# Balancing two batches by sums on ScalarE, with a new order of work from the start of mixing

## The chip, the cores and the metric

The kernel runs on one core of a Trainium2 chip. It uses TensorE (PE, matrix products), VectorE (DVE), ScalarE (ACT), GpSimd (POOL) and the queue of SyncE (SP), which starts most of the transfers. The metric is the device time of one execution in microseconds (us).

## The reference

All arrays are seeded random numbers; q, k, v are (4 batches, 4 heads, 1088 positions, 32), and the attention features come from two 8 x 32 matrices S1, S2.

```python
def phi(x):                                   # 64 features of each position
    a = np.einsum('rd,bhsd->bhsr', S1, x)
    b = np.einsum('rd,bhsd->bhsr', S2, x)
    return np.einsum('bhsi,bhsj->bhsij', a, b).reshape(*x.shape[:-1], r * r)
q_p, k_p = (phi(q), phi(k))
kv = np.einsum('bhsf,bhsd->bhfd', k_p, v)
z = np.sum(k_p, axis=2)
num = np.einsum('bhsf,bhfd->bhsd', q_p, kv)
den = np.einsum('bhsf,bhf->bhs', q_p, z)[..., None] + 1e-06
x = num / den                                 # then as (batch, position, 128)
theta = x @ w_theta
zr, zi = x * np.cos(theta), x * np.sin(theta)
y = w_tok_r @ zr + w_tok_i @ zi               # mixes the 1088 positions
u = x + y
out = u + np.maximum(u @ w_ch, 0.0)
```

## The kernel before

**Stages.** Positions are cut into chunks of 128 (nine, the last one short), 128 on the partitions. For each batch the kernel forms sums over keys ("keys", "sums", "rest"), a small chain of 32x32 and 128x128 products on them ("chain"), kv ("kf", "kv"), the scaled and rounded queries ("qT", "q0"), the two factors of the denominator ("levels", "den"), the numerator ("num"), theta with its cosine and sine ("theta"), and then mixes positions: w_tok stands as 17 rows of 128 x 1088 (eight real, eight imaginary, one with the ends of both), each loaded as 8-byte words into a buffer of class "zs" and turned into floats by two ScalarE activations (L576, L578) and two VectorE steps (L580, L582). Batches 0 and 1 are mixed row by row ("mix", L1197): for each row three products of up to 384 columns add into three PSUM banks. Batches 2 and 3 (PAIR) are mixed together by seven products of half matrices (function winograd, "m1" to "m7"), for which VectorE makes sums and differences of the w_tok rows and of the two batches' z. The last step, u + relu(u @ w_ch), and the stores are in finish.

**The join.** For batches 1 to 3 the keys k are taken apart into a rounded part kb and a rest r. The "rest" products (L680) are of r with k + kb. That sum, kh, is not made by an engine: k is loaded a second time into kh, and a transfer issued by POOL adds kb to it in place (function join, L326, called in key_sums, stage "keys"). There are 9 x 4 narrow products (32 columns on 32 output partitions); L682 then puts the result's two "corners" together by 32x32 products.

**The turn.** For batches 1 to 3 (XTURN) x is not transposed by PE: VectorE transposes 32x32 blocks (L1097), SP sends the result to a place in HBM ("far", L1098) and fetches it back in another order (L1102).

**The balance.** Before batches 2 and 3 are mixed together, batch 3 is scaled by a power of two near the ratio of the two batches' magnitudes, partition by partition. balance() (L1166) puts a magnitude of each batch into columns 0 and 1 of the tile even, takes the powers of two (ratio, L1172), and leaves the factor in column 4 and its inverse in column 5. ScalarE scales batch 3 by it ahead of its turn (L1092). Scaling and its inverse are both exact, so only the size of rounding errors hangs on the choice.

**What sets the order.** The functions do not issue instructions; they record 1001 operations with their engine, buffers and predecessors. The tuple ORDER lists all operations, and issue() emits them in that order; each engine then runs its own part of the list strictly in order and waits on semaphores where an input or a buffer is not ready. GAPS says where small idle products are put on PE as a filling, SLOTS which physical buffer each logical one takes: a buffer can be written only when the last user of the one before it in its place is through, so SLOTS adds waits of its own. "zs" has five places, which w_tok's raw rows, z, and the turn's tiles share. Mixing begins on PE at 57 us with rows 0, 1, 2 of batch 0.

Of the kernel before, what the change touches and what calls it, by code (L numbers as in the profile page):

```python
# [11 lines left out]
BF16 = mybir.dt.bfloat16  # L12
# [5 lines left out]
AF = mybir.ActivationFunctionType  # L18
ALU = mybir.AluOpType
AX = mybir.AxisListType  # L20
PSUM = bass.MemoryType.PSUM

P = 128
# [54 lines left out]
)  # L78
GAPS = {11: 3, 57: 3, 79: 3, 110: 1, 203: 8, 153: 1, 77: 5, 86: 2, 163: 1}
SLOTS = (  # L80
# [11 lines left out]
)  # L92
WARM = 0
LOAD_LEAD = 60.0
# [37 lines left out]
class Layout:  # L132
# [17 lines left out]
    def buf(self, cls, shape, dt, name):  # L150
        b = Buf(cls, shape, dt, name)
        self.bufs.append(b)
        return b
# [75 lines left out]
def dve(n):  # L229
    return (n + 145) / 960.0  # L230


def dve2(n):
    return (n / 2 + 150) / 960.0


def act(n):
    return 0.17 + 0.00083 * n
# [7 lines left out]
def kernel(  # L246
# [12 lines left out]
    B, _, NC, H, D = q.shape  # L259
# [38 lines left out]
    op, buf = L.op, L.buf  # L298

    def at(*name):  # L300
        L.stage = "".join(str(x) for x in name)

    V, A, G, T, SY = nc.vector, nc.scalar, nc.gpsimd, nc.tensor, nc.sync

    def fixed(shape, dt, name):
        b = Buf(None, shape, dt, name)
        n = math.prod(shape) * WORD[dt]
        b.ap = view(const.tile([P, (n + 3) // 4], F32, tag=name, name=name), shape, dt)
        return b
# [4 lines left out]
    def ts(o, a, s1, op0, s2=None, op1=None, eng=None):  # L314
        kw = {} if op1 is None else {"op1": op1}
        (eng or V).tensor_scalar(out=o, in0=a, scalar1=s1, scalar2=s2, op0=op0, **kw)  # L316

    def stt(o, a, s, b, op0, op1, eng=None):
        (eng or V).scalar_tensor_tensor(out=o, in0=a, scalar=s, in1=b, op0=op0, op1=op1)  # L319
# [8 lines left out]
    def vop(n, fn, w, r, due=None, two=False, lk=0):  # L328
        op("V", dve2(n) if two else dve(n), fn, w, r, due, lk=1 if two else lk)
# [80 lines left out]
    def powers(mfn, m, n, name):  # L410
# [7 lines left out]
        def inv():  # L418
# [16 lines left out]
                                    op=ALU.max, apply_absolute_value=True), [m2], [(sp, 0)])  # L435
# [476 lines left out]
    qs, qx, q0, xT, zt = {}, {}, {}, {}, {}  # L912
    even = fixed((6,), F32, "even")
# [109 lines left out]
    def outputs_x(b, lv, pool_qp):  # L1023
# [60 lines left out]
        if b == PAIR[1]:  # L1084
            src = balance()
# [80 lines left out]
    def balance():  # L1166
        at("even")
        for j, b in enumerate(PAIR):
            vop(NC * P, lambda j=j, b=b: V.tensor_reduce(out=even()[:, j:j + 1], in_=xT[b](), axis=AX.X, op=ALU.max,
                                                         apply_absolute_value=True), [(even, j)], [xT[b]])  # L1170

        def ratio():  # L1172
            e = even()
            ts(e[:, 0:2], e[:, 0:2], TINY, ALU.max, 1.0 / TINY, ALU.min)
            ei = e.bitcast(I32)
            ts(ei[:, 2:4], ei[:, 0:2], EXPO, ALU.bitwise_and, EXPO, ALU.bitwise_xor)
            ts(ei[:, 0:2], ei[:, 0:2], EXPO, ALU.bitwise_and)
            stt(e[:, 4:5], e[:, 0:1], 0.5, e[:, 3:4], ALU.mult, ALU.mult)
            stt(e[:, 5:6], e[:, 1:2], 0.5, e[:, 2:3], ALU.mult, ALU.mult)

        op("V", 0.85, ratio, [even], [], lk=5)
        return even
# [300 lines left out]
```

## Time and profile before

| | before |
|---|---|
| median of 3 runs | 217.91 us (217.88 to 218.24) |
| the profiled execution | 217.77 us |
| its span, first to last instruction | 216.0 us |
| granted TensorE clock, mean | 0.997 |
| busy: PE, DVE, ACT, POOL | 207.4, 180.7, 113.5, 38.5 us |
| moved by DMA | 37.06 MB |

A row of a timeline or of the chain has the start, the time it takes (both us), engine, line, operation, output and inputs, and their shapes; x says how many instructions or records are merged into it. A float32 product appears as two records. A row of groups ends in "busy us, mean ns | idle before". A matmul's end is modelled, and the records of consecutive products overlap: PE's real pace is the distance from start to start. Lines are those of the kernel before; the changed kernel has one line more from L1169 on.

### The profile page before, as it was taken

How to read it: one execution, taken by the hardware profiler on the slowest of the kernel's cores; microseconds unless marked ns; L12 is line 12 of the kernel's file. 1: busy time of each engine (PE TensorE's matmuls, PEld its weight loads, DVE VectorE, ACT ScalarE, POOL GpSimd, SP SyncE). 2: the span in 40 equal slices, each digit the busy share in tenths (PEclk: the TensorE clock that was granted, in tenths of full speed). 3: DMA queues.
4: the chain of work that ended last, by engine and by line, in shares of the span. 5: the costliest groups of instructions: out<-in, count | busy, mean ns of one | idle time of the engine just before them, and what ended most of it. 6: DMA issues, size and time to landing. Idle time of an engine off the chain costs nothing.

```text
span 216.0 us, 5299 instructions
## 1 busy us (share of the span) xinstructions
PE 207.4 (96%) x2140; PEld 150.2 (70%) x2140; DVE 180.7 (84%) x359; ACT 113.5 (53%) x240; POOL 38.5 (18%) x89
## 2 busy tenths in 40 slices
PE   7999999999999999999999999999999999999990
PEld 7777798968767666775656676576766776677660
DVE  1799999999999998998999999979497799955151
ACT  4899999999999896796711423159500000000000
POOL 1182640307300000930003010000220020020013
PEclk9999999999999999999999999999999999999998
DMA  6999999996996994192002244022660012110433
GB/s 226 395 417 418 380 362 420 429 324 143 347 244 230 421 429 177 56 323 49 0 0 36 40 141 113 0 39 108 137 109 0 0 39 50 17 36 4 76 62 67
DMA packets 28044, 37.06 MB, mean 172 GB/s; under 512 B 20564, under 2 KB 23044, under 8 KB 25844
## 3 DMA queue, kind: packets, MB, share of 16 engines
q1 hardware_dynamic: 22868, 31.86, 42.2%
q0 software_dynamic: 1552, 3.25, 7.1%
q10 hardware_dynamic: 3600, 1.62, 2.8%
q8 instruction: 17, 0.28, 0.5%
q14 instruction: 7, 0.06, 0.1%
HBM read 29.84 MB, written 4.00 MB: 157 GB/s over the span
## 4 chain that ended last, share of the span: by engine, by line
PE 58%; DMA 17%; DVE 10%; ACT 9%; issue 3%; SPq 1%; POOL 0%; POOLq 0%; DVEq 0%; ACTq 0%
PE ps L332 54%; DMA zs<-w_tok 11%; DMA zs<-far 2%; DMA st<-s 2%; DVE big L312 2%; ACT big L578 2%; PE ps L951 2%; ACT big L626 2%; DMA far<-zs 1%; DVE g L312 1%; PE ps L1053 1%; DVE big L316 1%; ACT g L726 1%; ACT big L576 1%; PE ps L361 1%
## 5 line engine op out<-in xcount | busy, mean ns | idle before, releaser
L332 PE MATMUL ps<-big,zs 128*128 128x384 f32 (+2 forms) x380 | 108.8, 435 | 0.0
L332 PEld LDWEIGHTS ps<-big,zs 128*128 128x128 f32 x380 | 67.1, 191 | 34.2 <-issue 0.9
L1281 ACT COPY g<-ps 80x256 f32<-80x256 f32 x1 | 0.4, 367 | 54.1 <-PE ps L1274 54.1
L332 PE MATMUL ps<-big,big 128*32 128x32 f32 (+2 forms) x352 | 21.8, 235 | 0.0
L312 DVE CUSTOM_DVE_ANT_0 big<-big,big 128x2176 uint16<-128x2176 uint16 x17 | 21.6, 1281 | 0.1
L578 ACT ACTIVATE big<-zs 128x1088 int32<-128x1088 uint32 (+1 forms) x18 | 21.3, 1190 | 0.7 <-DMA zs<-w_tok 0.7
L576 ACT ACTIVATE big<-zs 128x1088 f32<-128x1088 f32 x17 | 20.9, 1229 | 0.7 <-DMA zs<-w_tok 0.7
L332 PEld LDWEIGHTS ps<-big,big 128*32 128x32 f32 (+1 forms) x352 | 14.9, 125 | 5.6 <-issue 1.0
L312 DVE TENSOR_TENSOR big<-big,big 128x544 f32<-128x544 f32 x24 | 16.7, 713 | 0.1
L326 POOL DMA_DIRECT2D g<-big x6 | 5.3, 1070 | 56.0 <-ACT g L1213 56.0
L1236 POOL DMA_DIRECT2D out<-g x8 | 5.0, 631 | 50.3 <-DVE g L1240 36.0
L312 DVE TENSOR_TENSOR zs<-zs,g 128x384 f32<-128x384 f32 (+2 forms) x24 | 9.9, 449 | 4.0 <-DMA zs<-far 4.0
L316 DVE TENSOR_SCALAR big<-big 128x1088 int32<-128x1088 int32 x17 | 12.3, 721 | 0.0
L361 PE MATMUL ps<-idle 128*128 128x112 bf16 (+1 forms) x67 | 10.0, 312 | 1.3 <-POOL idle L363 1.3
L312 DVE TENSOR_TENSOR g<-lv 128x768 f32<-128x768 f32 x12 | 11.1, 950 | 0.1
L312 DVE TENSOR_TENSOR big<-big,hf 128x1152 f32<-128x1152 f32 x8 | 10.7, 1351 | 0.0
L332 PE MATMUL ps<-mf,big 128*128 128x96 f32 (+1 forms) x72 | 10.0, 278 | 0.4 <-DVE big L312 0.4
L332 PE MATMUL ps<-sbk,g 128*128 128x64 f32 x72 | 10.1, 276 | 0.3 <-ACT g L726 0.3
L332 PE MATMUL ps<-w,big 128*128 128x128 f32 (+1 forms) x76 | 10.2, 278 | 0.0
L332 PEld LDWEIGHTS ps<-w,big 128*128 128x128 f32 (+1 forms) x76 | 9.4, 190 | 0.5
L1139 ACT ACTIVATE g<-g 128x384 f32<-128x384 f32 x12 | 6.3, 532 | 6.7 <-DVE g L319 6.7
L332 PEld LDWEIGHTS ps<-sbk,g 128*128 128x128 f32 x72 | 9.0, 191 | 0.8 <-ACT g L726 0.6
(198 smaller groups left out, 353.0 us busy)
## 6 DMA issues: line engine op xcount, KB each, us to landing
zs<-w_tok SPq DMA_DIRECT2D x17, 1088.0 KB, 10.6
big<-k_l SPq DMA_DIRECT2D x5, 576.0 KB, 12.6
big<-v_l SPq DMA_DIRECT2D x4, 576.0 KB, 15.4
big<-q_l SPq DMA_DIRECT2D x3, 576.0 KB, 10.4
big<-hf POOLq DMA_DIRECT2D x3, 576.0 KB, 9.7
far<-zs SPq DMA_DIRECT2D x3, 576.0 KB, 3.8
zs<-far SPq DMA_DIRECT2D x12, 144.0 KB, 4.1
big<-k_l ACTq DMA_DIRECT2D x2, 576.0 KB, 4.2
```

The lines of the kernel that those rows point to most:

```text
L312: eng.tensor_tensor(out=o, in0=a, in1=b, op=f)
L316: (eng or V).tensor_scalar(out=o, in0=a, scalar1=s1, scalar2=s2, op0=op0, **kw)
L326: op("G", 0.9, lambda: G.dma_start(dst(), src(), accum_op=ALU.add), w, r, fly=fly)
L332: T.matmul(o, lhs, rhs, start=start, stop=stop, skip_group_check=True)
L361: T.matmul(nowhere()[:, :n], idle()[:, 0:P], idle()[:, :n], start=True, stop=True, skip_group_check=True)
L576: op("A", 0.22 + n * 0.0009, lambda: A.activation(dfn(), words_of(raw(), n)[1].bitcast(F32), AF.Prelu, scale=2.0**-112, alpha=-(2.0**32)), ...
L578: op("A", 0.22 + n * 0.0009, lambda: A.activation(stp(), words_of(raw(), n)[0].bitcast(U32), AF.Copy, scale=2.0**-29), [stp], [raw])
L626: op("A", act(n) + 0.1, lambda: A.activation(flat(r()), kc(), AF.Square, accum_out=km()[:, 1:2]), [r, (km, 1)], [kx])
L726: op("A", act(GW), lambda kT=kT, tr=tr: A.copy(kT().rearrange("p c n -> p (c n)"), tr()), [kT], [tr])
L951: T.transpose(tr()[:, i * P:(i + 1) * P], x()[:, g * GC + i].rearrange("p h d -> p (h d)"), ident())
L1139: op("A", act(GW), lambda cs=cs: A.activation(cs()[:, 0], cs()[:, 1], AF.Abs), [(cs, 0)], [(cs, 1)])
L1236: E.dma_start(out[b, s0:s0 + n, f * SQ:(f + 1) * SQ].rearrange("(c j) i -> j c i", j=SQ), ot()[f * SQ:(f + 1) * SQ, :n].rearrange("j (c i) ...
```

## The change

One part is in balance: in place of VectorE's largest magnitude of x along each partition stands ScalarE's sum of magnitudes, an activation Abs with an accumulated output, whose full output goes to a scratch tile of the class "hf".

```diff
         for j, b in enumerate(PAIR):
-            vop(NC * P, lambda j=j, b=b: V.tensor_reduce(out=even()[:, j:j + 1], in_=xT[b](), axis=AX.X, op=ALU.max,
-                                                         apply_absolute_value=True), [(even, j)], [xT[b]])
+            dump = buf("hf", (NC * P,), BF16, "dump")
+            op("A", act(NC * P) + 0.1, lambda j=j, b=b, dump=dump: A.activation(
+                dump(), xT[b](), AF.Abs, accum_out=even()[:, j:j + 1]), [dump, (even, j)], [xT[b]])
```

The other part is a new tail of ORDER (the first 399 entries stay, the other 602 are in a new order) and, with it, of SLOTS; the buffers that are in use by then keep their places. GAPS stays.

```diff
-    501, 489, 375, 538, 490, 378, 545, 502, 491, 292, 496, 261, 382, 546, 503, 498, 390, 393, 504, 547, 383, 401, 384,
-    377, 548, 416, 394, 505, 549, 282, 398, 406, 379, 493, 550, 229, 380, 397, 230, 231, 262, 232, 233, 234, 235, 293,
+    501, 489, 375, 538, 490, 378, 545, 502, 491, 292, 496, 261, 382, 503, 282, 498, 293, 546, 377, 547, 548, 302, 228,
+    393, 497, 299, 304, 383, 229, 549, 230, 231, 189, 550, 232, 493, 233, 551, 379, 552, 234, 345, 499, 553, 500, 294,
...
```

What that does engine by engine, in the lists as they are emitted (503 to 505 are rows 2 to 4 of batch 0; 229 to 237 batch 2's nine chunks of "rest", 293 the corners of batch 3, 239 those of batch 2; 493 a transposition in theta):

- PE before: rows 2, 3, 4 of batch 0, 493, 229 to 235 with one piece of kv 3 between, 293, 236, 237, a transposition, rows 5 to 8, then numerators of batch 1, kv 2 and the chain of batches 2 and 3.
- PE after: row 2, 293, 229 to 231, a transposition, 232, 493, 233, 234, row 3, 235 to 237, row 4, kv 3, 239, one group of transpositions, the chain's first products, row 5, all of batch 1's numerators and thetas, and then rows 6 and on. Three pieces of kv 2 stand apart from each other among rows of batches 0 and 1.
- PE's end before: the last row of product 3, two steps of batch 3 of 256 columns, a w_ch product of 160 columns of batch 2, and one of 384 columns of batch 3. After: product 4's 160-column part comes last, then the two 256-column steps, and the w_ch product of 160 columns of batch 2 is the last one; the 384 columns of batch 3 come some four us before it.
- SP before: raw rows 10, 13, 11, 15, 14, 12, the turn of batch 1, row 16 in between. After: rows 11, 10, 13, both parts of the turn of batch 1, then rows 15, 14, 12, 16.
- POOL keeps its order up to the chain of batches 2 and 3; its joins of "keys" stand where they stood.

68 rows, old and new, of tables (ORDER, SLOTS) are left out of this document.

## The prediction

> **What bounds the kernel now.** I read the page first, then busy time by stretches, PE's waits, the DMA view, PE's list from 61 us, and the last steps.
>
> ```profile
> span 216.0 us, 5299 instructions
> ...
> PE 207.4 (96%) x2140; PEld 150.2 (70%) x2140; DVE 180.7 (84%) x359; ACT 113.5 (53%) x240; POOL 38.5 (18%) x89
> ```
> ```profile
> 60.00:100.00 40.00, 39.63 (x436) 27.35 (x435) 37.22 (x62) 34.31 (x60) 6.74 (x13) 1.00 0.73 255
> 100.00:150.00 50.00, 49.54 (x341) 32.73 (x340) 47.07 (x81) 20.64 (x41) 2.68 (x3) 1.00 0.18 42
> 150.00:209.00 59.00, 59.00 (x256) 41.59 (x255) 41.60 (x87) 4.21 (x11) 5.79 (x8) 1.00 0.29 57
> ```
> In each stretch the columns are the length, then PE, PEld, DVE, ACT and POOL busy, the granted clock, and the DMA share. From 60 to 209 us TensorE is busy for 148.17 of 149 at clock 1.00: its products follow each other without holes, so the end is PE's work, its few stalls, and a tail. VectorE is almost full up to 150 (37.22 of 40, 47.07 of 50). After 60 us PE waits twice that the trace can name:
>
> ```profile
> PE ps L332 <- DVE big L312: 0.4, 1, 0.4
> PE ps L332 <- ACT sm L783: 0.4, 1, 0.4
> ```
> The modelled ends of the products before hide 0.1 of each, so they cost about 0.5 each, 1.0 together. A change in order can win this and something in the tail, not more; what it can lose is open.
>
> **The change, part by part.** The lists agree up to the third product row of batch 0 (w_tok row 2), on PE at 60.89.
>
> *Balance (L1169).* Two maxima leave VectorE; two activations with a sum come to ScalarE.
>
> ```profile
> L1169 DVE TENSOR_REDUCE even<-big 128x1 f32<-128x1152 f32 x2 | 2.7, 1330 | 0.8 <-ACT big L1081 0.8
> L626 ACT ACTIVATE big<-big 128x1152 f32<-128x1152 f32 x4 | 4.7, 1169 | 1.4 <-DMA big<-k_l 1.4
> L626 ACT ACTIVATION_READ_ACCUMULATOR big<-big 128x1 f32 x4 | 0.8, 198 | 0.0
> ```
> VectorE loses 2 x 1.33 = 2.7; ScalarE gains 2 x (1.17 + 0.20, overlapping by 0.1) = 2.5. ScalarE is busy for 20.64 of 50 there and the factor is wanted only for batch 3's turn, so neither stands on PE's path: 0. Were that cover gone, 1.3 (one activation) would come before batch 3's sines. Abs is already used between copies and sines, so I expect no new table load.
>
> *The join of batch 2's keys: the large term.* POOL adds the rounded keys to kh by a DMA (L326, from keys2); the 36 narrow products "rest2" (L680) read kh.
>
> ```profile
> 53.89 0.91 POOL L326 DMA_DIRECT2D big<-hf  x1
> ```
> ```profile
> big<-hf POOLq DMA_DIRECT2D x1, 576.0 KB, 11.2
> ```
> The second row is the DMA view of 53 to 56 us: this one issue took 11.2 us, so kh is there at 53.89 + 11.2 = 65.1. PE's list:
>
> ```profile
> 60.89 5.65 PE L332 MATMUL ps<-big,zs 128*128 128x384 f32 x18
> 66.37 0.49 PE L1126 MATMUL ps<-ident,big 128*128 128x128 f32 x3
> 66.79 0.40 PE L332 MATMUL ps<-big,big 128*32 128x32 f32 x24
> 67.00 0.52 PE L332 MATMUL ps<-g,big 128*32 128x64 f32 x24
> 67.34 0.48 PE L332 MATMUL ps<-big,big 128*32 128x32 f32 x32
> 67.75 0.26 PE L332 MATMUL ps<-ident,g 32*32 32x32 f32 x8
> 67.83 0.24 PE L332 MATMUL ps<-g,ident 32*32 32x32 f32 x8
> 68.01 0.33 PE L332 MATMUL ps<-big,big 128*32 128x32 f32 x16
> 68.27 0.33 PE L906 MATMUL ps<-ident,sm 128*128 128x128 f32 x1
> 68.44 0.49 PE L332 MATMUL ps<-big,zs 128*128 128x384 f32 x1
> ```
> Three product rows of batch 0 and a transposition fill 60.89 to 66.79; the first rest2 product then comes 1.7 after the join has landed and waits for nothing. In the changed order only one product row (row 2, 5.48 / 3 = 1.83) and batch 3's corners (67.75 to 68.01, 0.26, with its mode changes 0.35) stand ahead: PE is at rest2 at 60.89 + 1.83 + 0.35 = 63.1. All that leads to the join (POOL's list, SP's queue, the loads in flight) is the same, so PE, which takes its list in order, stands until 65.1: **+2.0**. Everything on PE queues behind it, and ScalarE's and VectorE's next steps (the level of the sums, the third sine part of theta) wait for those products in turn.
>
> The Trainium skill ("DMA: Bandwidth & Descriptors", Anatomy of one DMA) fits such a transfer as 2.0 us plus its bytes at 436 GB/s, 3.4 us here. By that the join would be in at 57.3, the wait would be 0 and the sum 217.2. The row has 11.2; the fit is for one DMA at a time, and here loads fill the engines, so the row decides.
>
> *Mode changes on PE.* Between full 128x128 products and narrow ones (128x32, 32x32, 128x64) PE loses time; the list above and this group show how much.
>
> ```profile
> L1126 PE MATMUL ps<-ident,big 128*128 128x128 f32 x9 | 1.5, 275 | 0.0
> ```
> Three L1126 transpositions begin 0.11 apart (one takes 275 ns, so the last starts at 66.86 - 0.275); the narrow one follows 0.20 after it: 0.10 lost. Eight narrow 128x32 records take 0.07 (24 from 66.79 to 67.00), but the 16 before 68.27 take 0.26: 0.12 lost. The full one after them takes 0.17 where 0.11 is usual: 0.06. So an excursion into narrow work costs 0.28. After 60.89 PE makes 6 excursions before: rest2 with the corner of batch 3; kv2 with corner and first chain product; two with batch 1's numerators; the two quads of batches 2 and 3. In the changed list I count 14: corner 3 with rest2's start, one and two rest2 chunks between a transposition and a product row, rest2's end, kv3 with corner 2, the chain's first product, three numerators, three single kv2, two quads. Eight more, of which the first hides half in the wait: 7.5 x 0.28 = 2.1; inside excursions there are three changes of kind fewer (0.12 each): -0.35. **+1.7**. The bounds are 0 (all of it hidden) and 2.4.
>
> The Trainium skill ("TensorEngine Tiling (Array Packing)", Key Properties) says that a change of tiling mode drains TensorE; the 0.28 agrees.
>
> *Stalls that go.* The chain product (after ScalarE L783) and batch 3's levels (after VectorE L312) stand behind inputs that are now ready 1 us and more ahead: **-1.0**. Late next, by adding each engine's rows in the new order and putting in each wait by hand: batch 3's quads want VectorE's last transposition (L1043). VectorE has 73.5 of work ahead of it from 60.25 and 7.0 of waits in eight places, so 140.8; PE comes at 141.2. 0.4 is the thinnest spare; the row products have 3.
>
> *Rows 15, 14, 12, 16* are moved in SP's queue behind the turn of batch 1, and share its buffers.
>
> ```profile
> zs<-w_tok SPq DMA_DIRECT2D x17, 1088.0 KB, 10.6
> ...
> big<-hf POOLq DMA_DIRECT2D x3, 576.0 KB, 9.7
> far<-zs SPq DMA_DIRECT2D x3, 576.0 KB, 3.8
> zs<-far SPq DMA_DIRECT2D x12, 144.0 KB, 4.1
> big<-k_l ACTq DMA_DIRECT2D x2, 576.0 KB, 4.2
> ...
> out<-g POOLq DMA_DIRECT2D x7, 48.0 KB, 2.2
> ...
> out<-g POOLq DMA_DIRECT2D x1, 20.0 KB, 1.9
> ```
> The turn is on VectorE at 80.5 by the same adding; with the ways out and back (3.8 and 4.1) and its issues it is back at about 90. Row 12 can be issued when row 15 has been read, at about 97.7. Bounds: 4.2 (half the bytes, quiet queues) to 10.6. The DMA share at that time is low (0.18 after 100), so I take 5: landed at 102.7, ScalarE 2.4, VectorE 1.9, ready at 108 against PE's 111. At 10.6 it would be 1.6 late. **0**, with 1.6 as its upper end.
>
> *The tail.* Before, the last product is 384 columns of batch 3 (209.49).
>
> ```profile
> 209.49 0.86 PE L332 MATMUL ps<-big,w 128*128 128x384 f32 x2
> ```
> ```profile
> 209.76 0.42 DVE L319 SCALAR_TENSOR_TENSOR g<-ps,g 80x256 f32<-80x256 f32 x1 [0.15 <-PE ps L332]
> 210.11 0.33 DVE L1240 STREAM_TRANSPOSE g<-big 128x160 f32<-128x160 f32 x1
> 210.38 0.56 DVE L319 SCALAR_TENSOR_TENSOR big<-ps,big 128x384 f32<-128x384 f32 x1
> ```
> ```profile
> 210.73 0.59 POOL L1236 DMA_DIRECT2D out<-g  x1 [3.93 <-DVE g L1240]
> 211.85 1.24 POOL L1236 DMA_DIRECT2D out<-g  x2 [0.52 <-DVE g L1240]
> ```
> From 209.49 to the end are 6.5. Now those 384 columns go earlier and 160 columns of batch 2 come last. From that product's start: 0.9 until the 80x256 step is through, 0.4 more for the two 160-column steps, the second of 0.33 (1.3), 0.29 to POOL, one issue of 0.59: 2.2. From POOL's last issue (213.1) to the end were 2.9; 20 KB land 0.3 sooner than 48 KB: 4.8 in all. The 384 columns (0.69 of PE) are now ahead and the 160 (0.27) behind: 4.8 + 0.4 - 6.5 = **-1.3**.
>
> Sum: 2.0 + 1.7 - 1.0 - 1.3 = +1.4. The profiled execution is 217.77, 1.77 outside its span, and 0.14 under the median of the runs shown (217.91): 217.77 + 1.4 = **219.2**.
>
> **The rivals.**
> *The join costs nothing (faster).* Were kh there by 63.1, 9.2 after its issue, the 2.0 falls away: 217.2. For it speaks that 9.7 is the median of the three joins; against it that this one took 11.2 with the same neighbours. It decides at 63.1; from 64.8 on the kernel is slower.
> *Mode changes cost little.* If other delays on PE hide most of the 1.7: 217.5 to 218.2, within 0.2%. For it: the 0.28 is read from one place. Against: PE has no slack in which to hide it.
> *A further wait.* Row 12 or 16 lands late, or batch 3's quads wait: 1.6 more, 220.8. For it: thin spare behind two serial loads. Against: low DMA shares.
> *The sum on ScalarE does not take the place of the maximum in time* (it starts later, behind sines): batch 3's factor comes up to 1.3 later; products that need it begin 10 us after. No change in the sum; no chance of its own.
>
> **How the numbers follow.** Forecast 0.60 (its own range 218.5 to 220.2: mode changes from 1.0 to 2.4, tail +-0.3), join free 0.12, mode changes little 0.12, further wait 0.16. The 2 in 10 left out are the low half of the free join and the ends beyond 221.0; the range is 217.4 to 221.0. About 0.2% (0.44 us) is what a measurement of this kernel can tell from none: faster 0.12, same 0.12, slower 0.76.
>
> **What would show it.** In PE's waits of the changed kernel a new line of about 2.0 on L332, released by the DMA big<-hf, at 63.1 to 65.1; the two lines of 0.4 gone; TENSOR_REDUCE of L1169 gone from VectorE and two activations on ScalarE near 133 and 144; the last PE product 160 wide at about 212.7; POOL's last issue alone. Wrong would be: no idle time of PE at 63, product rows waiting for DMA zs<-w_tok by way of VectorE near 111, or a tail of over 5.5.

## The result, and the profile after

The changed kernel takes 219.39 us (median of 11 runs) where the kernel before takes 218.11 beside it: a ratio of 1.0066, 95% interval 1.0041 to 1.009. It is slower by 0.4 to 0.9%, and 219.39 lies 0.2 above the forecast. Its runs spread from 218.70 to 221.40, three of them at 220.8 or more, where those beside it spread from 217.65 to 218.24; no trace shows one of the three. The profiled execution took 219.6; its span is 217.8, against 216.0 before. First the page, the three stretches (length, then PE, PEld, DVE, ACT and POOL busy, clock, DMA share, GB/s) and the first line of PE's waits, all of the changed kernel:

```profile
span 217.8 us, 5293 instructions
...
PE 209.5 (96%) x2140; PEld 150.8 (69%) x2140; DVE 179.1 (82%) x357; ACT 116.0 (53%) x244; POOL 38.2 (18%) x89
```
```profile
60.00:100.00 40.00, 38.23 (x403) 25.36 (x402) 36.94 (x66) 31.73 (x59) 6.40 (x13) 1.00 0.59 200
100.00:150.00 50.00, 50.00 (x365) 33.03 (x364) 43.56 (x71) 22.64 (x38) 3.57 (x4) 1.00 0.29 86
150.00:209.00 59.00, 59.00 (x245) 40.69 (x244) 42.25 (x86) 7.50 (x16) 4.30 (x6) 1.00 0.28 56
```
```profile
PE ps L332 <- ACT sm L778: 1.8, 1, 1.8
```
Before 100 us PE now stands for 1.8, at one place; after 100 it never stands, where before it lost 0.46. Its two waits of 0.4 are gone. VectorE is busy for 1.6 us less than before and ScalarE for 2.5 more; the two sums of the balance are on ScalarE, where the forecast had them:

```profile
L1170 ACT ACTIVATE hf<-big x2: 1156/1160/1163, 133.5 to 144.8; 128x1152 bf16<-128x1152 f32 x2
```
(The row has the durations in ns, least, median and most, and the first and last start.) PE's list around the new wait:

```profile
57.34 5.75 PE L332 MATMUL ps<-big,zs 128*128 128x384 f32 x18
63.02 0.26 PE L332 MATMUL ps<-ident,g 32*32 32x32 f32 x8
63.10 0.24 PE L332 MATMUL ps<-g,ident 32*32 32x32 f32 x8
65.11 0.40 PE L332 MATMUL ps<-big,big 128*32 128x32 f32 x24 [1.77 <-ACT sm L778]
65.44 0.33 PE L906 MATMUL ps<-ident,sm 128*128 128x128 f32 x1
65.70 0.27 PE L332 MATMUL ps<-big,big 128*32 128x32 f32 x8
65.89 0.55 PE L1126 MATMUL ps<-ident,big 128*128 128x128 f32 x3
66.37 0.33 PE L332 MATMUL ps<-big,big 128*32 128x32 f32 x16
66.63 2.10 PE L332 MATMUL ps<-big,zs 128*128 128x384 f32 x6
68.66 0.40 PE L332 MATMUL ps<-big,big 128*32 128x32 f32 x24
68.98 1.24 PE L332 MATMUL ps<-big,zs 128*128 128x384 f32 x3
```
PE is through with batch 3's corners (63.10 + 0.24), then stands, and starts the first rest2 product at 65.11. POOL's list, the DMA view of 54 to 55 us, and ScalarE's list say what it stood for:

```profile
54.09 0.91 POOL L326 DMA_DIRECT2D big<-hf  x1
```
```profile
big<-hf POOLq DMA_DIRECT2D x1, 576.0 KB, 10.9
```
```profile
63.07 0.17 ACT L676 COPY g<-ps 128x32 f32<-128x32 f32 x1
...
64.72 0.31 ACT L778 ACTIVATE sm<-g,kg 128x32 f32<-128x32 f32 x1
```
The join is issued at 54.09 and lands 10.9 later, at 65.0. In the trace PE's product waits on two semaphores: that transfer's, complete at 65.0, and a count of ScalarE's steps. The page names L778, whose row ends at 65.03, merely because it is ScalarE's last row before PE starts; nothing that this product reads comes from it. The ScalarE step in the list that the product must follow is the copy of batch 2's sums (L676), done at 63.24. So by these rows the wait belongs to the join; the experiments check that.

The tail, from the last product on:

```profile
212.89 0.46 PE L332 MATMUL ps<-big,w 128*128 128x160 f32 x2
213.14 0.42 DVE L319 SCALAR_TENSOR_TENSOR g<-ps,g 80x256 f32<-80x256 f32 x1 [0.39 <-PE ps L332]
213.48 0.31 DVE L319 SCALAR_TENSOR_TENSOR big<-ps,big 128x160 f32<-128x160 f32 x1
...
213.83 0.34 DVE L1241 STREAM_TRANSPOSE g<-big 128x160 f32<-128x160 f32 x1
...
214.47 0.60 POOL L1237 DMA_DIRECT2D out<-g  x1 [1.58 <-DVE g L1241]
```
From 212.89 to the end of the span are 4.9, against 6.5 from the last product before.

**Where the 1.8 us are.** The starts of PE's records, one after the other, give a sum in both traces. From the first product of mixing (57.13 before, 57.34 after) to the last product's start (209.49, 212.89) PE takes 3.19 longer. 0.42 of it is that 384 columns and not 160 now stand ahead of the last product. The wait at 63.3 is 1.8. The stalls of before at 78.7, 117.8 and 100 give back 1.2 (0.46, 0.58 and 0.20, each start against the usual step). What is left, 3.19 - 0.42 - 1.8 + 1.2 = 2.2, lies in steps of 0.1 at changes between full and narrow products; added up one by one, these steps too come to 2.2 more than before. The tail gives 0.42 - (6.5 - 4.9) = -1.2. With 0.2 by which mixing began later (there the lists agree, so that is scatter), 1.8 + 2.2 - 1.2 - 1.2 + 0.2 = 1.8. This sum is of one execution of each kernel; the medians are 1.3 apart.

### The profile page after: what moved, and what is told of

It is laid out like the page before. It is cut to its first block, busy times and chain, and to the rows that moved or that the text cites. A ratio compares the mean times of both kernels' runs of the same rounds, so it can differ in the third digit from the quotient of the medians.

```text
span 217.8 us, 5293 instructions
## 1 busy us (share of the span) xinstructions
PE 209.5 (96%) x2140; PEld 150.8 (69%) x2140; DVE 179.1 (82%) x357; ACT 116.0 (53%) x244; POOL 38.2 (18%) x89
## 4 chain that ended last, share of the span: by engine, by line
PE 79%; ACT 13%; DMA 2%; issue 2%; DVE 1%; POOL 1%; POOLq 0%; SPq 0%; ACTq 0%
PE ps L332 73%; DMA st<-s 2%; ACT big L576 2%; ACT big L578 2%; PE ps L1053 2%; PE ps L951 2%; ACT big L626 2%; ACT g L726 1%; PE ps L361 1%; ACT g L1140 1%; POOL out L1237 1%; ACT g L1136 1%; ACT lv L991 1%; ACT g L1142 1%; ACT g L1139 1%
## 5 line engine op out<-in xcount | busy, mean ns | idle before, releaser
L332 PEld LDWEIGHTS ps<-big,big 128*32 128x32 f32 (+1 forms) x352 | 14.4, 124 | 6.8 <-ACT sm L778 1.8
L319 DVE SCALAR_TENSOR_TENSOR big<-ps,even,big 128x160 f32<-128x160 f32 (+1 forms) x10 | 4.9, 490 | 6.1 <-PE ps L332 6.1
```

The costliest lines, as they stand in the source:

```text
L332: T.matmul(o, lhs, rhs, start=start, stop=stop, skip_group_check=True)
```

## The experiments

All ratios are to the kernel before, run beside the kernel on the same chip.

**The wait: three edits.** *row3_first* puts one product row ahead of the rest2 products:

```diff
-    ... 299, 304, 383, 229, 549, ...   294, 504, 235, ...
+    ... 299, 304, 383, 504, 229, 549, ...   294, 235, ...
```


> The changed order with one entry moved: row 3 of batch 0 (504) stands on PE ahead of the first rest2 product (229), so that PE comes to 229 at about 65.2 instead of 63.3. Theory (the wait on PE at 63.3 is for the join of batch 2's keys, landing at 65.0): the wait of 1.8 goes, nothing takes its place, 219.4 - 1.8 = 217.6. Rival 1 (the wait is for ScalarE's L778, which the page names, or for another step that would come as late): PE waits the same 1.8 two us later or at another product, 219.4. Rival 2 (a stall further down takes the gain back, since VectorE is then later against PE): over 218.6.

Measured: 218.05, ratio 1.0011 (0.9994 to 1.0027). PE's list and the new line in its waits:

```profile
63.19 2.10 PE L332 MATMUL ps<-big,zs 128*128 128x384 f32 x6
65.22 0.40 PE L332 MATMUL ps<-big,big 128*32 128x32 f32 x24
```
```profile
PE ps L1053 <- DVE sm L312: 0.4, 1, 0.4
```
The rest2 product starts at 65.22, nearly as in the changed kernel (65.11), though PE has done a row meanwhile; so it was not PE's own work that had set its start there. Rival 1 is not yet out, since L778 too was done by then. Of the 1.8, 0.4 comes back at 69.8, where batch 1's first numerator now waits for VectorE. The span is 216.2, 1.6 shorter.

*join_early* leaves PE's list alone and issues the join on POOL ahead of the step (186) for which POOL otherwise waits until 49.9:

```diff
-    ... 274, 275, 250, 186, 40, ...   482, 485, 218, 537, ...
+    ... 274, 275, 250, 218, 186, 40, ...   482, 485, 537, ...
```


> The changed order with one entry moved: POOL's join for batch 2 (218) stands ahead of the step that POOL waits for until 49.9 (186) instead of three steps behind it. Its copy of k was asked for at 36.5, so the join can be issued at some time between 41 and 50. Theory (the join's place in POOL's list sets its landing): issued 4 us or more earlier it lands by 61, PE does not wait at 63.3: 219.4 - 1.8 = 217.6. Rival (the landing is set by the loads that fill the DMA engines until 65, whenever the join is issued): the wait stays, 219.4; a part of both if it lands between 61 and 65.

Measured: 217.98, ratio 0.9995 (0.9963 to 1.0027); span 216.2. POOL's list, PE's and ScalarE's:

```profile
51.10 0.86 POOL L326 DMA_DIRECT2D big<-hf  x1 [10.17 <-DMA big<-k_l]
```
```profile
63.23 0.24 PE L332 MATMUL ps<-g,ident 32*32 32x32 f32 x8
63.44 0.40 PE L332 MATMUL ps<-big,big 128*32 128x32 f32 x24
```
```profile
64.92 0.31 ACT L778 ACTIVATE sm<-g,kg 128x32 f32<-128x32 f32 x1
```
POOL waits for the copy of k until 51.1, so the join could come only 3.0 earlier, less than the 4 that I had expected; at about 10 us it lands near 61. That is enough: PE goes from the corners to rest2 with no wait in the page. ScalarE's second L778 starts at 64.92, after PE has begun: L778 is out, and since only the join was moved, its landing was the cause of the wait.

*wait_into_before* puts the wait into the kernel before, by taking rows 3 and 4 from ahead of rest2:

```diff
-    ... 503, 498, 390, 393, 504, 547, ...   394, 505, 549, ...   189, 426, 506, ...
+    ... 503, 498, 390, 393, 547, ...   394, 549, ...   189, 426, 504, 505, 506, ...
```


> The kernel before with one thing of the changed order alone: rows 3 and 4 of batch 0 (504, 505) stand behind the rest2 group on PE, not ahead of it; no excursion into narrow products is added. Theory: PE stands from about 63.0 until the join lands at 65.1, 2.0 more: 218.1 + 2.0 = 220.1, with up to 0.5 given back if the later stall at 78.7 shrinks. Rival (a wait there is made up for later, since other stalls shrink as PE is later): under 219.0.

Measured: 218.98, ratio 1.0038 (1.0009 to 1.0067); span 217.3, 1.3 longer.

```profile
PE ps L332 <- DMA big<-hf: 1.6, 1, 1.6
```
Here the page names the join. The wait came where the theory has it (1.6 for 2.0); its cost did not. From the first product of mixing to the last one's start PE takes 153.3, against 152.4 before: 0.9 more (the other 0.3 of the span is a later start of mixing), and the ratio says 0.8 (0.2 to 1.5). So 220.1 was 1.1 too high, and 218.98 lies just under the 219.0 that the rival had named: about 0.7 of the 1.6 is made up for later. The stalls at 78.7 (ScalarE's L783, 0.5) and at 100 (0.2) are gone. That they went because PE comes later is not shown: in *tail_alone*, below, both are gone too, though its lists are those of the kernel before up to there.

**The price of a mode change.** Added zeros in the last stage of the kernel before, where PE waits for nothing; a first attempt added nothing, and so timed the kernel before twice more:

```diff
+        def poke(o, n):
+            for _ in range(n):
+                for h in range(H):
+                    u, v = (slice(x * D, (x + 1) * D) for x in (h, (h + 1) % H))
+                    mm(o()[u, :D], ident()[u, v], ident()[u, u], False, False)
...
                         mm(ps()[:, :w], zz[0](i, i + 1)[:, 0], aa[0](i)[:, c0:c1], fresh and i == 0, i == n - 1)
+                        if j == 0 and name in "56734" and 0 < i < 7:    # narrow_spread
+                            poke(ps, 1)
+                        if j == 0 and name == "5" and i == 3:           # narrow_grouped (a run of its own)
+                            poke(ps, 30)
```


> The kernel before with work added: after each of 30 full products of the last stage (products 5, 6, 7, 3, 4, their 384-column part, i from 1 to 6) four 32x32 products of zeros are added into the same bank, so that nothing changes but time. 30 more excursions into narrow products, in the stretch where PE waits for nothing. The work itself is 8 records in 0.08 us: 2.4 for 30. Theory (0.28 an excursion with its work, 0.20 without): 217.8 + 2.4 + 30 x 0.20 to 0.28 = 226.2 to 228.6. Rival (mode changes are hidden by the weight loads): as narrow_grouped, 220.4.

> The same 30 x 4 added products of zeros, all after one full product (product 5, i = 3): the same work with one excursion. Both theories: 217.8 + 2.4 + 0.2 = 220.4. The difference from narrow_spread over 29 is the price of a mode change out and back: 0.20 to 0.28 by the first theory, near 0 by the rival.

Measured: 217.46, ratio 0.9991 (0.9963 to 1.0019), and 218.21, ratio 0.9998 (0.9968 to 1.0028). When the lines are called, j is the loop's last value, so no product was added; the expectations do not apply. With `c0 == 0` in place of `j == 0`:

> narrow_spread and narrow_grouped timed the kernel before itself, since their added lines asked for a loop variable that had moved on when they were called; here they ask for the part's first column. The kernel before with work added: after each of 30 full products of the last stage (products 5, 6, 7, 3, 4, their 384-column part, i from 1 to 6) four 32x32 products of zeros are added into the same bank. Theory (0.28 an excursion with its work, 0.20 without): 217.8 + 2.4 + 30 x 0.20 to 0.28 = 226.2 to 228.6. Rival (mode changes are hidden by the weight loads): as narrow_grouped2, 220.4.

> The same 30 x 4 added products of zeros, all after one full product (product 5, i = 3): the same work with one excursion. Both theories: 217.8 + 2.4 + 0.2 = 220.4. The difference from narrow_spread2 over 29 is the price of a mode change out and back: 0.20 to 0.28 by the first theory, near 0 by the rival.

Measured: 229.73, ratio 1.0522 (1.0483 to 1.0561), and 224.36, ratio 1.0257 (1.0223 to 1.0292). First PE's list of the kernel before, then of narrow_spread2:

```profile
171.90 0.81 PE L332 MATMUL ps<-big,big 128*128 128x384 f32 x2
172.54 0.44 PE L332 MATMUL ps<-big,zs 128*128 128x160 f32 x2
```
```profile
172.05 0.81 PE L332 MATMUL ps<-big,big 128*128 128x384 f32 x2
172.79 0.26 PE L332 MATMUL ps<-ident 32*32 32x32 f32 x8
172.98 0.91 PE L332 MATMUL ps<-big,big 128*128 128x384 f32 x2
173.82 0.26 PE L332 MATMUL ps<-ident 32*32 32x32 f32 x8
```
A 384-column product gives way to the next after 0.64. Here the narrow ones come after 0.74 (0.10 lost), take 0.19 until the next full product (0.07 is their work, 0.12 is lost), and that product takes 0.84 (0.10 lost). An excursion (into narrow products and back) costs 0.32, and 0.39 with its work; all 30 of this trace have the same steps and make 11.7, and the medians are 11.2 apart. That is 1.1 over the top of what I had expected (228.6), which was worked out with at most 0.28 each. The rival, that weight loads hide the changes, is out. narrow_grouped2 was to take 2.6 more and took 5.9:

```profile
166.08 1.75 PE L332 MATMUL ps<-ident 32*32 32x32 f32 x184
170.04 0.69 PE L332 MATMUL ps<-ident 32*32 32x32 f32 x56 [2.21 <-issue]
170.66 0.91 PE L332 MATMUL ps<-big,zs 128*128 128x384 f32 x2
```
240 narrow records take 4.6, of which 2.2 is a hole after 184 of them, in which PE waits for nothing that the profile shows. Without it they take 2.4, as expected. So the difference of the two medians (5.4, or 0.19 for each of 29) is too low a price: with the hole added back it is 0.26, from medians of four runs each, whose traces also differ in a stall at 100 (2.0 and 1.1). The rows' 0.32, where PE waits for nothing, is the better figure.

*rest_grouped* takes changes away from row3_first's order: 189 and 493 ahead of the corners, rest2's nine products in one piece, kv2's 202 and 208 in one piece, and ScalarE's copy 228 ahead of them:

```diff
-    503, 282, 498, 293, 546, 377, 547, 548, 302, 228, 393, 497, 299, 304, 383, 504, 229, 549, 230, 231, 189, 550, 232, 493, 233, ...
+    503, 189, 493, 282, 498, 228, 293, 504, 229, 230, 231, 232, 233, 234, 235, 236, 237, 546, 377, 547, 548, 302, 393, ...
-    202, 649, 626, 208,
+    202, 208, 649, 626,
```


> The order of row3_first with fewer changes between full and narrow products on PE: the transpositions 189 and 493 stand ahead of batch 3's corners, the nine rest2 products (229 to 237) follow one another, and kv2's pieces 202 and 208 do too. Three excursions into narrow work fewer. Theory (0.28 each): row3_first was 218.05; 0.84 less, 217.2, and the waits as there. Rival (the mode changes cost little, the rest of the 2.0 that PE's list lost is something else): 218.0.

Measured: 216.74, ratio 0.995 (0.9925 to 0.9974); span 214.8, 1.4 under row3_first's.

```profile
63.52 2.10 PE L332 MATMUL ps<-big,zs 128*128 128x384 f32 x6
65.55 0.83 PE L332 MATMUL ps<-big,big 128*32 128x32 f32 x72
66.31 2.10 PE L332 MATMUL ps<-big,zs 128*128 128x384 f32 x6
```
The steps at the changes are 0.84 less, 0.28 for each of the three excursions, and row3_first's wait of 0.4 at L1053 is gone too, which I had not expected; the last 0.1 is an earlier start of mixing. This kernel is faster than both: by 0.3 to 0.75% than the one before.

**The tail alone**, in the kernel before (900 to 904 and 916 earlier, 995 last; VectorE's steps follow):

```diff
-    984, 978, 914, 989, 900, 990, 901, 902, 985, 986, 903, 991, 993, 987, 904, 915, 919, 920, 992, 964, 988, 995, 921, 905, ..., 916, ...
+    978, 900, 901, 914, 902, 903, 904, 915, 905, 989, 990, 991, ..., 981, 982, 983, 984, 916, 985, 986, 987, 917, 918, 988, 919, 921, 920, 922, 995, ...
```


> The kernel before with the end of the order alone rearranged as in the changed kernel: the last row products of product 3 (900 to 904) come ahead of product 4's 160-column part, the w_ch product of batch 3's 384 columns (916) several products earlier, and the 160 columns of batch 2 (995) last. Theory (what follows the last product is 4.9 in the changed kernel and 6.5 before, and the last product is 0.4 shorter): 217.8 - 1.2 = 216.6. Rival (the end is set by the stores before, not by the last product's size): 217.8.

Measured: 217.05, ratio 0.9975 (0.9952 to 0.9998); span 215.0, 1.0 shorter. Of this 1.0 only half is the tail: the end of the span comes 5.6 behind the last product's start (6.5 before, 4.9 in the changed kernel), so the tail gives 0.42 - (6.5 - 5.6) = -0.5, and the ratio says the same. The other half is that the stalls at 78.7 and 100 are missing, in a stretch where the lists are those of the kernel before. So the tail works, but gives less than half of the 1.2 expected. ScalarE's queue in the tail, and the steps behind it:

```profile
207.50 2.05 ACTq L1236 DMA_DIRECT2D out<-g  x2
...
209.45 0.54 PE L332 MATMUL ps<-big,w 128*128 128x160 f32 x2
...
209.59 0.37 ACT L1281 COPY g<-ps 80x256 f32<-80x256 f32 x1 [55.26 <-DMA out<-g]
209.99 0.42 DVE L319 SCALAR_TENSOR_TENSOR g<-ps,g 80x256 f32<-80x256 f32 x1 [0.59 <-PE ps L332]
```
ScalarE issues stores from 207.50 to 209.55 and can copy only then, so VectorE's step follows the last product's start by 0.54, where it is 0.25 in the changed kernel (212.89, 213.14). That is 0.3 of the 0.7 between 5.6 and 4.9; the other 0.4 comes after POOL's last issue (211.31, to the end 3.7; 3.3 in the changed kernel), and its cause is open.

**The balance.** *balance_alone* is the kernel before with the diff's new balance and its order unchanged (the two scratch tiles take places 0 and 2 of "hf").

> The kernel before, its order kept, with the new balance alone: two sums on ScalarE in place of two maxima on VectorE. Theory: off PE's path on both engines, 218.1, within 0.4 of the kernel before. Rival 1 (VectorE, which is nearly full there, is what PE waits for at 117.8 or later, and gains 2.7): 217.6 or less. Rival 2 (the sum stands in ScalarE's list ahead of steps of batch 2 and holds them): 218.7 or more.

Measured: 217.50, ratio 0.9981 (0.995 to 1.0011): no difference that can be told. (217.50 lies under the 217.6 of rival 1, but the kernel before took 217.81 beside it, and from the first product of mixing to the last one's start PE takes 151.6 here and 151.6 in *narrow_spread*, which is the kernel before.) *old_balance_new_order* is the changed order with the two maxima of VectorE.

> The changed order with the old balance: VectorE's two maxima stand where the two sums of ScalarE stand in the list. In the changed kernel VectorE is through with the last transposition for batch 3's quads at 141.3 and PE comes to them at 141.9; the first maximum stands ahead of that transposition and takes 1.3. Theory (the spare of 0.5 is all there is): PE waits 0.8 at the quads, 219.4 + 0.8 = 220.2. Rival (VectorE has idle time ahead of it in which the maximum fits): 219.4.

Measured: 219.74, ratio 1.0078 (1.0046 to 1.011). VectorE's and PE's lists:

```profile
130.68 1.34 DVE L1169 TENSOR_REDUCE even<-big 128x1 f32<-128x1152 f32 x1
...
140.61 0.96 DVE L1043 STREAM_TRANSPOSE zs<-g 128x768 f32<-128x768 f32 x1
```
```profile
141.62 1.60 PE L332 MATMUL ps<-zs,g 32*32 32x288 f32 x64 [0.23 <-DVE zs L1043]
```
PE waits 0.2, not 0.8. In this execution VectorE started its stretch 0.5 earlier and the maximum used up 0.4 of its idle time, so the transposition ends only 0.25 later than in the changed kernel. At 219.74 and 219.39 the two balances cannot be told apart in this order either.

## Why the prediction was right, step by step

- **The total: right, in part by luck.** The +1.4 was worked out for the profiled execution, whose span grew by 1.8: 0.2 is scatter, and the four terms measured 1.8 + 2.2 - 1.2 - 1.2 = 1.6. The medians differ by 1.3. That 219.39 is so near 219.2 is in part luck, with runs from 218.7 to 221.4; the direction and the terms are not.
- **The join: right in place and cause, 0.2 off in size.** 1.8 in place of 2.0: PE came at 63.34 and not 63.1, and the join landed at 65.0. The sign that I had named was wrong: the page puts the wait down to ScalarE's L778. What settles it are row3_first, join_early and wait_into_before. By the Trainium skill's fit for one transfer ("DMA: Bandwidth & Descriptors", Anatomy of one DMA) an estimate for this one is 3.4; here it took 10.9.
- **Mode changes: right, undersized by 0.5.** The trace has the 14 excursions that I counted. 7.5 x 0.28 - 0.35 was 1.7; with narrow_spread2's 0.32 for each it is 2.05, and the trace has 2.2. What I had missed is the first full product after the narrow ones, which loses 0.10 and not 0.06 when it has 384 columns. The Trainium skill says that a change of tiling mode drains PE ("TensorEngine Tiling (Array Packing)", Key Properties); narrow_spread2's 0.32 agrees with that, though no row shows the draining itself.
- **Stalls that go: right in this pair of traces.** 1.2 for 1.0; the 0.2 is a stall at 100 that I did not list. How large these stalls are changes from one execution of the same list to the next (see the end). The thin spare held: VectorE's transposition for batch 3's quads ends at 141.3 and PE comes at 141.9 (forecast 140.8 and 141.2).
- **Row loads: right.** In the changed kernel the loads of rows 14, 12 and 16 took 5.2 (I took 5), row 12 was ready at 109.4 (forecast 108, though my own terms, 102.7 + 2.4 + 1.9, add up to 107.0), and PE used it at 111.8.
- **Tail: right.** -1.2 for -1.3. Inside it two sizes were off and cancelled: the 80x256 step was through 0.7 after the last product's start and not 0.9, and the two steps of 160 columns took 0.6 more and not 0.4. tail_alone shows that the kernel before gets only 0.5 from the same rearrangement.
- **Balance: right**, 0 within what can be told, in both orders. (VectorE's busy time fell by 1.6 and not by the two maxima's 2.7; why is open.)
- **Rivals.** "The join costs nothing" is refuted by the wait and by join_early, and "mode changes cost little" by narrow_spread2 and rest_grouped; the "further wait" did not come. Two bounds do not follow from their terms: with 217.2 and no wait up to 63.1, the time passes 217.91 by 0.44 when the join lands at 64.2, not 64.8; and 218.5, the low end of the forecast's own range, leaves out the tail's 0.3 (218.2 with it).

## What to carry to other kernels

When an engine that is the bound reads a transfer, look up that transfer's landing and put as much independent work ahead of its first reader as the gap needs: one entry moved was worth 0.5 to 0.7% here. On PE, count each excursion into narrow products and back as work of about 0.3 us, and gather the narrow products. A new order that wins in one place (here the tail and the stalls, 2.4) can lose more in another; a sum over the starts of PE's records shows both. A stall of a few tenths in one trace is worth a second trace of the same list before it is counted as a gain.

## What was not expected

- narrow_grouped2's hole of 2.2 after 184 narrow records on end, put down to "issue". Its cause is open. The DMA view of 164 to 172 us has two 16 KB transfers of the queue "instruction", one of them from 167.4 to 168.7, in the hole; that PE had run out of instructions is a guess which no run tests.
- The stall at 100 in the kernel before is not a fixed cost. PE waits there for VectorE, which in narrow_spread2 itself waits 2.8 for batch 1's turn to come back (the transfer zs<-far). Over the seven traces whose lists agree up to there, PE stands there for nothing (tail_alone, balance_alone, narrow_spread), 0.2 (the kernel before), 1.1 (narrow_grouped2), 1.8 (narrow_grouped) and 2.0 (narrow_spread2). PE's waits in the last of these have the line

```profile
PE ps L332 <- DVE zs L312: 1.9, 1, 1.9
```
The five traces with the new order, which starts that turn earlier, have no stall there. So the new order may win more by this than one trace of the kernel before can show; how much, no run settles.
